# An S4D convolution with a routed MLP: merged loads for the last 64 channels of the gate and up weights, and products of constants ahead of the blocks that finish the last two channel groups

## The chip, the cores and the metric

The kernel runs on one core of one Trainium2 chip. The core has a matrix engine (TensorE, PE in the profile, with its weight loads on a row PEld), a vector engine (VectorE, DVE), a scalar engine (ScalarE, ACT), a general engine (GpSimd, POOL), and a sync engine (SyncE, SP) that only issues transfers; 16 DMA engines move data between HBM and the on-chip memory SBUF of 128 rows. TensorE writes to the eight banks of PSUM. The metric is the device time of one execution in microseconds; lower is better.

## The reference, cut to what matters

```
L, D, N, F = 2048, 576, 128, 4608
mod = (silu(c) @ w_mod)                       # sa, ca, ga, sb, cb, gb: six rows of 576
h = layernorm(x) * (1 + ca) + sa
# first half: S4D, a long convolution of every channel along the 2048 positions
A = -exp(log_A_real) + 1j * A_imag ;  dt = exp(log_dt) ;  C = (C_real + 1j * C_imag) * dt
K = 2 * einsum("dn,dnl->dl", C, exp(A * dt * pos)).real      # one filter per channel
y = irfft(rfft(h.T, 4096) * rfft(K, 4096))[:2048].T + h * D_skip
x = x + ga * y
# second half: a SwiGLU MLP for the 8 tokens with the highest router score
h = layernorm(x) * (1 + cb) + sb
r = h @ w_r ;  idx = argsort(-r)[:8] ;  s = h[idx]
z = ((silu(s @ w_gate) * (s @ w_up)) @ w_down) * sigmoid(r[idx])
x = x + gb * (h with z added at rows idx)
```

w_gate and w_up are 576 x 4608, w_down is 4608 x 576, all in 32-bit floats.

## The kernel before, in words

The 576 channels are worked in five groups, four of 128 channels and one of 64 (`GS`). For each group the filter is built, and the convolution is done as a two-level Fourier transform with TensorE products. Function `conv` (L944 on) multiplies the spectra of one part of a group and transforms back on one level (L1020); the copies at L1027 bring the result, z, from PSUM to a tile `zs`, and a store puts it into the DRAM tensor `dZ` (L1030). Function `y_group(g, jb)` then finishes quarter `jb` of the positions of group `g`: two loads bring z back from `dZ` in another order into a tile `zr` (L1052), eight TensorE products with the constant `g1` turn it into positions (L1061, 16 instructions in the trace, since each product is two passes), and VectorE adds the result to the residual `hx` (written by the helper `tt`, so the trace shows it at L342 as `hx<-b,hx`). There are two buffers of `zr`, so a load waits for the products of the block two before. When groups 2 and 4 are done, statistics (L1072) and sums for the router (L1079, L1092 on POOL, L1096 on ACT) follow for each quarter.

Then come the second normalization (`norm2`, small VectorE steps), the choice of the eight tokens (L1331 to L1367), the gathering of their rows (`px`, L1386, and L1409) into the tile `xT`, and the MLP: L1476 for gate and up, L1489 for a transpose, L1504 for down. Beside it, `base` scales all rows by the normalization and stores them (tiles `zr` again and `hx`, stores at L1455 on ACT's queue, four stores of 32 rows each for two token columns); its first four pairs use TensorE (L1449, L1450). At the end a scatter adds the MLP's rows (L1518).

The weights of the MLP are 45 tiles of up to 128 rows x 1536 numbers: for each of three parts s of F, four tiles each of gate and up with 128 channels (`g`, `u`), and one, `x`, that holds the last 64 channels of gate in rows 0 to 63 and those of up in rows 64 to 127; then 18 of w_down (`d`). `load_w` issues them on SP's queue in this order into 24 slots (`SLOTS`). The last eleven slots (`w2`) can only be filled when the convolution's memory is free, and the first of these loads also waits for the two small copies on POOL at L1139. An `x` tile is filled by two transfers (L1129, L1130).

The order of the work on each engine is written by a planner (`Plan`) from costs that stand in the code; the tables of priorities in `ORDER` belong to it. Each step has a planned cost and PSUM banks by name; a bank goes to a step in the planner's order, and on the chip the step waits until the bank's last reader is done. The change alters no planned cost, so the order stays. Waits on the chip are by semaphores; an engine works its list in order.

Of the kernel before, what the change touches and what calls it, by code (L numbers as in the profile page):

```python
# [310 lines left out]
def layouts(x):  # L311

    f = np.ascontiguousarray
    par = np.stack([x[n].T for n in ("A_C_real", "A_C_imag", "A_A_imag", "A_log_A_real")], 1)
    ld = np.zeros((128, NDT), np.float32)
    ld[:64] = x["A_log_dt"].reshape(64, NDT)
    dsk = np.zeros((128, KB, 4), np.float32)
    dsk[::32] = x["A_D_skip"].reshape(KB, 4, 4).transpose(2, 0, 1).reshape(4, KB, 4)
    cw = np.zeros((640, 1 + 6 * D), np.float32)
    cw[:D, 0], cw[:D, 1:] = x["c"][0], x["w_mod"]  # L320
    cw = cw.reshape(5, 128, 1 + 6 * D).transpose(1, 0, 2)
    return {"u": f(x["A_u"][0].reshape(32, 4, 16, D).transpose(1, 0, 2, 3).reshape(128, 16, D)),
            "par0": f(par[:, :, 0:GS[0]]), "par1": f(par[:, :, GS[0]:]),
            "head": f(np.concatenate([ld, cw[:, :, 0], dsk.reshape(128, 4 * KB)], 1)),
            "wm": f(cw[:, :, 1:].reshape(128, 5, 6, D).transpose(2, 0, 1, 3)),
            "wr": x["B_w_r"], "wg": x["B_w_gate"], "wu": x["B_w_up"], "wd": x["B_w_down"]}


@with_exitstack
def adaln_s4d_mod_kernel(ctx, tc, u, par0, par1, head, wm, wr, wg, wu, wd, cs, cfg, cr, cmv, out):  # L330
    nc = tc.nc
    V, S, P, T, Q = nc.vector, nc.scalar, nc.gpsimd, nc.tensor, nc.sync
    AX = mybir.AxisListType.X
# [66 lines left out]
    def banks(shape, names):  # L400
        return [ps.tile(shape, F32, name=nm) for nm in names]
# [4 lines left out]
    csm = const.tile([128, 128 + 128 + 32 + 16 + 1], F32, name="csm")  # L406
    ident = csm[:, 0:128]
# [538 lines left out]
    def conv(g, dp):  # L946
# [76 lines left out]
        for a in range(2):  # L1023
# [8 lines left out]
            ZS[x].rearrange("p (k e) -> p k e", e=n)), r=[("zsp", x, 0), ("zsp", x, 1)], inst=[("zs", x)],  # L1032
           w=[("dZ", g, dp)], dma=225, tag=f"y{g}")

    def y_group(g, jb):
        n = GS[g]
        gs = slice(GO[g], GO[g] + n)
        last = g >= G - 2
        if n == 128:
            ring("zr", (g, jb), 2)  # L1040
        elif not jb:
            ring("zr", (g, 0), 2)
            ring("zr", (g, 1), 2)
        jz = jb if n == 128 else jb // 2
        for m in range(2):
            s0 = 12 - 4 * jb if m == 0 else 4 * jb

            def lz(e, m=m, s0=s0):
                if (g, jz) not in ZT:
                    ZT[g, jz] = POOLS["z"].tile([128, 2, D], F32, name="zr", bufs=2)  # L1050
                ZR[g, jb, m] = flat(ZT[g, jz][:, m] if n == 128 else ZT[g, jz][:, jb % 2, 4 * n * m:4 * n * m + 4 * n], 4, n)
                (S if last and (n == 128 or not m) else Q).dma_start(ZR[g, jb, m], dZ[g][m, s0:s0 + 4].rearrange("s c h k e -> (c h k) s e"))  # L1052
            LX["z", g, jb] = op("A" if last and (n == 128 or not m) else "Q", .5, lz, r=[("dZ", g, dp) for dp in range(n // 16)],
                                w=[("zrp", g, jb, m)], inst=[("zr", (g, jz))], dma=290 if n == 128 else 190)
        st = {}

        def f(e, nm):
            st["p"] = py = banks([128, 4, n], nm)[0]
            for j4 in range(4):
                for m in range(2):  # L1060
                    T.matmul(py[64 * m:64 * m + 64, j4], g1[:, m], ZR[g, jb, m][:, 3 - j4 if m == 0 else j4],  # L1061
                             start=True, stop=True)
        m = op("T", .9 if n == 128 else .55, f, mode="1h", r=["csm"] + [("zrp", g, jb, m) for m in range(2)],
               inst=[("zr", (g, jz))], bank=1)
        op("V", vc(4 * n), lambda e: tt(hx[:, 4 * jb:4 * jb + 4, gs], st["p"], hx[:, 4 * jb:4 * jb + 4, gs], OP.add), uses=[m],
           w=[("y", g, jb)])
        if g not in (2, 4):
            return
        i, c0, c1 = (0, 0, 384) if g == 2 else (1, 384, D)
        yr = [("y", x, jb) for x in range(3 * i, g + 1)]  # L1070
        for j in range(4 * jb, 4 * jb + 4):
            op("V", vc(c1 - c0), lambda e, j=j: V.bn_stats(st2[:, j, i], hx[:, j, c0:c1]), r=yr, w=[("st2", i, j)])  # L1072

            def rd(e, j=j):
                yj = POOLS["z"].tile([128, 384], F16, name="yj")
                stt(yj[:, 0:c1 - c0], hx[:, j, c0:c1], 1.0, vrow[:, c0:c1], OP.mult, OP.mult,
                    accum_out=racc[:, j, i:i + 1])
            if i and j % 2 or not i and j < 8:
                op("V", vc(c1 - c0) + .13, rd, r=yr + ["vrow"], w=[("racc", i, j)], lock=True)  # L1079
                continue  # L1080
            kr = ring("pq", j, 2) if i else ring("pj", j, 1)
            sj = {}

            def pm_(e, j=j, sj=sj):
                if i:
                    if "pq" not in ZT:
                        ZT["pq"] = POOLS["z"].tile([128, 384], F32, name="pj", bufs=1)
                    sj["t"] = ZT["pq"][:, 192 * (j // 2 % 2):192 * (j // 2 % 2) + 192]
                else:
                    sj["t"] = POOLS["z"].tile([128, 384], F32, name="pj", bufs=1)  # L1090
                tt(sj["t"], hx[:, j, c0:c1], vrow[:, c0:c1], OP.mult, P)
            op("P", .6 if i else 1.08, pm_, r=yr + ["vrow"] + [("racc", 0, x) for x in range(8, 16)] * i, w=[("pj", i, j)], inst=[kr],  # L1092
               lock=True)

            def am_(e, j=j, sj=sj):
                S.activation(sj["t"], sj["t"], AF.Copy, accum_out=racc[:, j, i:i + 1])  # L1096
            op("A", ac(c1 - c0) + .12, am_, r=[("pj", i, j)], w=[("racc", i, j)], inst=[kr])
# [6 lines left out]
    def load_w(i):  # L1104
        s_, nm, k = key = order[i]
        sl = SLOTS[i % len(SLOTS)]
        rk = ring(sl, ("w", i), SLOTS.count(sl))

        def f(e):
            if sl[:2] == "sp":  # L1110
                w = spx[:, 1536 * int(sl[2]):1536 * int(sl[2]) + 1536]
            elif sl == "E":
                w = tw.tile([128, 3, 512], F32, name="E", bufs=NE).rearrange("p a d -> p (a d)")
            elif sl == "SC":
                w = tw.tile([128, 2, 2, 512], F32, name="SC", bufs=2).rearrange("p a b d -> p (a b d)")[:, 0:1536]
            else:
                w = W.pop("h", None) or W[sl].tile([128, 1536], F32, name="w")
            wtile[key] = w
            if nm == "d":
                f0 = 1536 * (k // 2) + 512 * s_ + 256 * (k % 2)  # L1120
                Q.dma_start(w[:, 0:2 * D].rearrange("p (r n) -> p r n", n=D),
                            wd[f0:f0 + 256].rearrange("(r p) n -> p r n", r=2))
                return
            w = w.rearrange("p (c x) -> p c x", c=3)

            def cols(x, r0, r1):
                return x[r0:r1].rearrange("p (c s x) -> p s c x", c=3, s=3)[:, s_]
            if nm == "x":
                Q.dma_start(w[0:64], cols(wg, 512, 576))  # L1129
                Q.dma_start(w[64:128], cols(wu, 512, 576))  # L1130
            else:
                Q.dma_start(w, cols(wg if nm == "g" else wu, 128 * k, 128 * k + 128))
        if i == SLOTS.index("w2"):
            r_ = [("zrp", G - 1, jb, m) for jb in range(4) for m in range(2)]

            def hold(e):
                W["h"] = W[sl].tile([128, 1536], F32, name="w")
                for n_ in range(2):
                    P.tensor_copy(W["h"][0:1, 8 * n_:8 * n_ + 8], ZR[G - 1, 3, n_][0:1, 0, 0:8])  # L1139
            op("P", .3, hold, r=[sl] + r_[6:], w=[("w", key)], inst=[rk, ("zr", (G - 1, 1))])  # L1140
        op("Q", .9 if nm == "x" else .45, f, r=[sl] if sl[0] == "w" else [], w=[("w", key)], inst=[rk],
           dma=495 if nm == "d" else 670)
        WK[key] = rk
# [47 lines left out]
    for x in (4, 3, 5):  # L1191
# [10 lines left out]
       w=["wrow"], **lk)  # L1202
# [29 lines left out]
    for b in range(KB):  # L1232
# [8 lines left out]
        g = group(b)  # L1241
# [101 lines left out]
    def pc(e, nm):  # L1343
# [5 lines left out]
       w=["i2"])  # L1349
# [5 lines left out]
       w=["pos", "jk"], lock=True)  # L1355
# [4 lines left out]
       w=["rsel", "jk"], lock=True)  # L1360
    op("A", .25, lambda e: S.activation(ft("rcol", [128, 1]), pk(2), AF.Sigmoid, bias=sc2[:, 1:2]), r=["rsel", "wrow"],
       w=["rcol"], table="sig")
    op("V", .1, lambda e: V.tensor_copy(ft("icol", [128, 1], I32), pk(1)), r=["idp"], w=["icol"])

    def pb(e, nm):
# [6 lines left out]
       w=["oh8"])  # L1372
# [90 lines left out]
    for s_ in range(3):  # L1463
# [22 lines left out]
        def tr(e, nms, st=st):  # L1486
# [5 lines left out]
           w=[("hT", s_)])  # L1492
# [19 lines left out]
    for c in range(4):  # L1512
# [6 lines left out]
        out=out[0], out_offset=bass.IndirectOffsetOnAxis(ap=ft("icol", None)[0:8, :1], axis=0), in_=ft("yo0", None)[0:8],  # L1519
# [24 lines left out]
```

## Time and profile before

| | |
|---|---|
| median of 3 runs | 483.56 us (483.1 to 487.92) |
| profiled execution | 484.27 us |
| its span, first to last instruction | 482.5 us |
| mean granted TensorE clock | 0.928 |
| busy: PE, PEld, DVE, ACT, POOL | 408.1, 285.2, 357.2, 318.7, 241.8 us |
| read from HBM, written | 71.94 MB, 23.62 MB |

A row of the timeline gives the start in us from the span's first instruction, the length, engine, line, operation, output and inputs, shape, a count, and in brackets how long the engine had been idle and what ended that. `SPq` and `ACTq` are issues of transfers on these engines' queues. A row of the windows gives for a stretch its length, each engine's busy time with the count of instructions, the granted TensorE clock (1.00 is full), the share of the DMA engines' time that was busy, and GB/s. In names like `b` (PSUM), buffer numbers are left out. Line numbers are those of the kernel before.

### The profile page before, as it was taken

The numbers are of one execution on the slowest core, as the hardware profiler recorded it, in microseconds if no ns is written. First come the engines' busy times: TensorE is split into PE (matmuls) and PEld (weight loads), VectorE is DVE, ScalarE is ACT, GpSimd is POOL, SyncE is SP. The second block draws the span as 40 slices with busy tenths as digits, with TensorE's granted clock in tenths as the row PEclk, the third lists the DMA queues.
The fourth block names the chain that finished last, engine by engine and source line by source line (L and its number), as shares of the span: only waits on it lengthen the run. The fifth ranks groups of instructions, "written<-read, shape, count | busy, mean of one in ns | idle before, by whom it ended". The sixth has DMA issues, their size and how long they took to land. (4 is left out here: it accounts for less than half of the span.)

```text
span 482.5 us, 15984 instructions
## 1 busy us (share of the span) xinstructions
PE 408.1 (85%) x6757; PEld 285.2 (59%) x6757; DVE 357.2 (74%) x751; ACT 318.7 (66%) x600; POOL 241.8 (50%) x206
## 2 busy tenths in 40 slices
PE   2968579969979889998899999999999869979474
PEld 1634335434547566866577777688798757543153
DVE  6898986899767877678896679688797859864121
ACT  5598966664897999999899989876622222252210
POOL 0006633022055788947758699956545533213931
PEclk9998966898999999999999999999999966998869
DMA  8995000476669522206432322575999777999993
GB/s 319 436 375 203 1 1 2 126 194 170 186 197 350 204 90 90 67 24 176 154 95 73 100 82 88 167 241 154 316 311 343 254 197 277 335 349 337 410 401 110
DMA packets 73388, 96.58 MB, mean 200 GB/s; under 512 B 12251, under 2 KB 45403, under 8 KB 72166
## 3 DMA queue, kind: packets, MB, share of 16 engines
q1 hardware_dynamic: 63686, 85.06, 53.8%
q10 hardware_dynamic: 9600, 10.49, 6.3%
q8 instruction: 53, 0.87, 0.8%
q14 instruction: 17, 0.14, 0.1%
q0 software_dynamic: 32, 0.02, 0.0%
HBM read 71.94 MB, written 23.62 MB: 198 GB/s over the span
## 5 line engine op out<-in xcount | busy, mean ns | idle before, releaser
L342 POOL TENSOR_TENSOR SC<-SC,E 128x1024 f32<-128x1024 f32 x36 | 86.1, 2394 | 98.6 <-ACT SC L851 54.4
L342 POOL TENSOR_TENSOR t<-t 128x256 f32<-128x256 f32 x72 | 55.1, 769 | 28.9 <-DVE t L342 23.3
L342 POOL TENSOR_TENSOR E<-E,SC 128x1024 f32<-128x1024 f32 x23 | 54.8, 2382 | 11.6 <-PE b L636 7.4
L342 DVE TENSOR_TENSOR t<-b,us 128x512 f32<-128x512 f32 x72 | 47.0, 685 | 12.6 <-PE b L970 9.6
L336 DVE TENSOR_SCALAR n<-b 128x512 f16<-128x512 f32 x72 | 46.9, 682 | 8.0 <-PE b L821 7.9
L844 ACT ACTIVATE SC<-b 128x512 f32<-128x512 f32 x72 | 42.1, 604 | 11.8 <-PE b L892 5.2
L1020 PE MATMUL b<-t,fg 64*128 64x128 f32 (+1 forms) x640 | 44.9, 281 | 2.9 <-issue 1.1
L1020 PEld LDWEIGHTS b<-t,fg 64*128 64x128 f32 x640 | 39.7, 187 | 9.1 <-issue 6.0
L795 ACT ACTIVATE E<-b 128x512 f32<-128x512 f32 x72 | 40.5, 606 | 3.4 <-PE b L791 3.2
L846 ACT ACTIVATE SC<-b 128x512 f32<-128x512 f32 x72 | 41.8, 598 | 0.2
L970 PE MATMUL b<-xk,fg 128*64 128x128 f32 (+1 forms) x640 | 38.5, 267 | 1.6 <-ACT zs L1027 0.8
L970 PE MATMUL b<-xu,fg 128*64 128x128 f32 (+1 forms) x640 | 37.3, 265 | 2.9 <-issue 1.0
L892 PE MATMUL b<-Bc,SC 128*32 128x64 f32 x1152 | 36.7, 224 | 1.8 <-DVE s L771 0.7
L970 PEld LDWEIGHTS b<-xk,fg 128*64 128x64 f32 x640 | 31.7, 137 | 10.5 <-issue 3.6
L342 POOL TENSOR_TENSOR zr<-zr,ksb 128x576 f32<-128x576 f32 x14 | 20.4, 1470 | 33.6 <-ACT zr L1435 27.0
L970 PEld LDWEIGHTS b<-xu,fg 128*64 128x64 f32 x640 | 32.2, 137 | 8.4 <-issue 1.8
L1435 ACT ACTIVATE zr<-hx,rs 128x576 f32<-128x576 f32 x16 | 12.9, 859 | 35.6 <-DMA out<-zr 16.8
L892 PE MATMUL b<-E,SC 128*32 128x64 f32 x1152 | 35.9, 222 | 0.3 <-DVE E L342 0.3
L912 PE MATMUL b<-csf,ksb 128*64 128x128 f32 x576 | 35.4, 275 | 0.3 <-DVE Bc L339 0.2
L892 PEld LDWEIGHTS b<-Bc,SC 128*32 128x32 f32 x1152 | 27.0, 111 | 12.6 <-issue 7.7
L912 PEld LDWEIGHTS b<-csf,ksb 128*64 128x64 f32 x576 | 31.2, 137 | 4.7 <-issue 1.5
L342 DVE TENSOR_TENSOR Bc<-E,b 128x512 f32<-128x512 f32 x36 | 24.5, 681 | 11.6 <-PE b L892 3.6
(251 smaller groups left out, 906.5 us busy)
## 6 DMA issues: line engine op xcount, KB each, us to landing
dX<-xs SPq DMA_DIRECT2D x32, 288.0 KB, 4.0
xu<-dX SPq DMA_DIRECT2D x36, 256.0 KB, 3.8
wt<-in_wm SPq DMA_DIRECT2D x6, 1440.0 KB, 15.1
w<-in_wu SPq DMA_DIRECT2D x9, 768.0 KB, 9.2
w<-in_wd SPq DMA_DIRECT2D x11, 576.0 KB, 8.6
w<-in_wg SPq DMA_DIRECT2D x8, 768.0 KB, 7.1
dZ<-zs SPq DMA_DIRECT2D x24, 256.0 KB, 2.3
zr<-dZ SPq DMA_DIRECT2D x24, 256.0 KB, 4.6
```

The source lines that it names most:

```text
L336: (eng or V).tensor_scalar(o, a, s1, s2, op0=op0, **({"op1": op1} if op1 is not None else {}))
L342: (eng or V).tensor_tensor(o, a, b, op=op)
L795: op("A", .49, lambda e, h=h: S.activation(tile_()[:, 1 + h], st["p"][h], AF.Exp), uses=[m], w=[("E", b, 1 + h)], inst=[("E", b)], table=" ...
L844: op("A", .49, lambda e, h=h: S.activation(sct()[:, h, 0], B_[h], AF.Abs), uses=[mm_[h]], r=[("ph", b, h)], w=[("ab", b, h)], inst=[("SC", ...
L846: op("A", .49, lambda e, h=h: S.activation(sct()[:, h, 1], B_[h], AF.Sin, scale=TWO_PI), uses=[mm_[h]], r=[("ph", b, h), ("ab", b, h)], w= ...
L892: T.matmul(kp[32 * t4:32 * t4 + 32, x], sc()[:, h, ri, 0, 32 * i:32 * i + 32], mo[ri][:, h, :, 32 * i:32 * i + 32], start=ri == 0, stop=ri ...
L912: T.matmul(o[64 * cc:64 * cc + 64, :, 4 * x:4 * x + 4].rearrange("p k j -> p j k"), ksb[:, b % KS, x], c1k[:, cc], start=True, stop=True)
L970: T.matmul(p[64 * a:64 * a + 64, q, cc], f2(k0 + k)[:, cc], src(k), start=True, stop=True)
L1020: T.matmul(pz[a][:, q], g2(k0 + 2 * q + cc)[r], pr[r, q, cc], start=cc == 0, stop=cc == 1, tile_position=(64 * a, 0))
L1435: op("A", ac(576), lambda e, j=j: S.activation(tile_(j), hx[:, j], AF.Identity, bias=rs[:, j, 1:2], scale=rs[:, j, 0:1]), r=[("rs2", j), ( ...
```

## The change

Two things are changed. The host lays out the last 64 channels of gate and up once more as an input `wx` of shape 3 x 128 x 1536, in the order in which an `x` tile holds them, and `load_w` fills an `x` tile by one transfer of 128 rows with 6144 contiguous bytes each instead of two transfers of 64 rows with three pieces of 2048 bytes each. And in `y_group`, for groups 3 and 4, three products (group 3) or two (group 4) of the constant identity with the first 256 columns of the constant tile `csm` are written into the block's PSUM tile before its eight products, which then overwrite it.

```diff
 def layouts(x):
     f = np.ascontiguousarray
+    runs = lambda w: f(w.reshape(-1, 3, 3, 512).transpose(2, 0, 1, 3).reshape(3, -1, 1536))
...
-            "wr": x["B_w_r"], "wg": x["B_w_gate"], "wu": x["B_w_up"], "wd": x["B_w_down"]}
+            "wr": x["B_w_r"], "wg": x["B_w_gate"], "wu": x["B_w_up"], "wx": runs(np.concatenate([x["B_w_gate"][512:], x["B_w_up"][512:]])), "wd": x["B_w_down"]}
...
+    def fill(p, n):
+        T.matmul(p.rearrange("p a b -> p (a b)")[:, 0:n], ident, csm[:, 0:n], start=True, stop=True)
+
     def y_group(g, jb):
...
         def f(e, nm):
             st["p"] = py = banks([128, 4, n], nm)[0]
+            for x in range((3 if n == 128 else 2) if g > 2 else 0):
+                fill(py, 256)
             for j4 in range(4):
                 for m in range(2):
                     T.matmul(py[64 * m:64 * m + 64, j4], g1[:, m], ZR[g, jb, m][:, 3 - j4 if m == 0 else j4],
...
+            if nm == "x":
+                Q.dma_start(w, wx[s_])
+                return
             w = w.rearrange("p (c x) -> p c x", c=3)

             def cols(x, r0, r1):
                 return x[r0:r1].rearrange("p (c s x) -> p s c x", c=3, s=3)[:, s_]
-            if nm == "x":
-                Q.dma_start(w[0:64], cols(wg, 512, 576))
-                Q.dma_start(w[64:128], cols(wu, 512, 576))
-            else:
-                Q.dma_start(w, cols(wg if nm == "g" else wu, 128 * k, 128 * k + 128))
+            Q.dma_start(w, cols(wg if nm == "g" else wu, 128 * k, 128 * k + 128))
```

More of the change, by code (lines that the diff above doesn't have):

```diff
@@ L325, in layouts, with adaln_s4d_mod_kernel @@
             "wm": f(cw[:, :, 1:].reshape(128, 5, 6, D).transpose(2, 0, 1, 3)),
-            "wr": x["B_w_r"], "wg": x["B_w_gate"], "wu": x["B_w_up"], "wd": x["B_w_down"]}
+            "wr": x["B_w_r"], "wg": x["B_w_gate"], "wu": x["B_w_up"], "wx": runs(np.concatenate([x["B_w_gate"][512:], x["B_w_up"][512:]])), "wd": x["B_w_down"]}
 @with_exitstack
-def adaln_s4d_mod_kernel(ctx, tc, u, par0, par1, head, wm, wr, wg, wu, wd, cs, cfg, cr, cmv, out):
+def adaln_s4d_mod_kernel(ctx, tc, u, par0, par1, head, wm, wr, wg, wu, wx, wd, cs, cfg, cr, cmv, out):
     nc = tc.nc
```

## The prediction

> **What bounds the kernel now.** I read the chain of waits first, from its end backwards. The profiled execution took 484.27 us around a span of 482.5, so 1.77 us lie outside the span.
>
> ```profile
> 384.14 1.05 PE b L1061 x16
> 410.26 0.88 ACT zr L1435
> 422.86 5.86 DMA out<-zr
> 433.25 4.45 PE b L1476 x32
> 437.72 8.44 DMA w<-in_wd
> 463.75 10.17 DMA w<-in_wd
> 473.94 3.51 DMA out<-hx
> ```
>
> Columns: start, length, what. Three stages are seen. To about 400 us the products of L1061 and the additions behind them end the last two groups. From 410 to 433 a chain of small steps runs the second normalization and the choice of the tokens, with stores of `out` in it (5.86 us for one). From 437.72 to the end it is weights arriving. So I ask two things: when does the tail at L1061 end, and how fast do weights flow after 437. The windows answer the second. The columns end with granted clock, DMA share and GB/s:
>
> ```profile
> 362.00:366.00 4.00, 4.00 (x80) 3.65 (x78) 3.45 (x7) 0.82 (x3) 2.34 (x4) 1.00 1.04 230
> 410.00:414.00 4.00, 2.86 (x18) 1.76 (x16) 2.81 (x9) 3.14 (x4) 1.88 (x2) 1.00 1.05 213
> 414.00:419.00 5.00, 4.95 (x17) 2.79 (x17) 4.33 (x14) 0.00 (x0) 0.94 (x1) 1.00 1.04 385
> 436.00:442.00 6.00, 6.00 (x80) 2.09 (x76) 2.08 (x3) 0.87 (x1) 2.80 (x2) 0.93 0.96 274
> 442.00:470.00 28.00, 18.23 (x271) 9.46 (x267) 7.71 (x11) 7.53 (x11) 16.09 (x11) 0.76 1.04 403
> ```
>
> The DMA engines are full in all five, but they move 385 to 403 GB/s in two and 213 to 274 in the others. The slow ones follow the issues of the half-tiles, whose two loads (L1129, L1130) each write 64 of the 128 rows:
>
> ```profile
> 399.40 0.55 SPq L1132 DMA_DIRECT2D w<-in_wu  x1
> 402.34 0.67 SPq L1129 DMA_DIRECT2D w<-in_wg  x1
> 403.06 0.60 SPq L1130 DMA_DIRECT2D w<-in_wu  x1
> 434.49 0.55 SPq L1129 DMA_DIRECT2D spx<-in_wg  x1
> ```
>
> Full tiles are cut in the same pieces of 512 numbers (L1132), so I blame the 64 rows, not the piece.
>
> For the first question, TensorE in the tail (start, length, idle before it and releaser):
>
> ```profile
> 384.07 1.09 PE L1061 MATMUL b<-zr,csm 128*64 128x128 f32 x16
> 386.33 1.09 PE L1061 MATMUL b<-zr,csm 128*64 128x128 f32 x16 [1.17 <-issue]
> 389.01 1.92 PE L1061 MATMUL b<-zr,csm 128*64 128x128 f32 x16 [1.58 <-DMA zr<-dZ]
> 391.71 2.46 PE L1061 MATMUL b<-zr,csm 128*64 128x128 f32 x16 [0.79 <-DVE hx L342]
> 394.95 1.98 PE L1061 MATMUL b<-zr,csm 128*64 128x64 f32 x32 [0.78 <-DVE hx L342]
> 398.15 1.98 PE L1061 MATMUL b<-zr,csm 128*64 128x64 f32 x32 [1.23 <-DMA zr<-dZ]
> ```
>
> The first four rows are the four blocks of group 3, the last two hold two blocks each of group 4. The same 16 instructions take 1.09 us, then 1.92 and 2.46: the granted clock halved.
>
> ```profile
> 385.70:389.11 3.41, 1.20 (x18) 1.01 (x20) 3.38 (x9) 1.23 (x4) 1.46 (x2) 1.00 0.78 238
> 389.11:406.18 17.07, 13.76 (x108) 10.84 (x108) 11.03 (x43) 4.26 (x18) 6.17 (x11) 0.50 0.70 200
> 409.59:413.01 3.42, 2.28 (x17) 1.53 (x16) 2.19 (x9) 2.75 (x4) 1.05 (x1) 1.00 1.06 229
> 430.08:433.49 3.41, 1.51 (x20) 0.88 (x16) 2.28 (x6) 2.51 (x4) 1.07 (x1) 1.00 0.76 234
> 433.49:436.90 3.41, 3.41 (x28) 1.23 (x24) 3.05 (x7) 0.98 (x2) 1.59 (x2) 0.50 1.03 360
> ```
>
> After a stretch with TensorE busy 1.20 of 3.41 us (35%) or 1.51 (44%) the clock is at 0.50; after one with 2.28 (67%) it stayed.
>
> **The change: the added products.** One product of the identity with 256 columns is priced by its like, with 288 columns at full clock:
>
> ```profile
> 406.38 0.65 PE L1449 MATMUL b<-ksb,csm 128*128 128x288 f32 x2
> 406.87 0.65 PE L1450 MATMUL b<-hx,csm 128*128 128x288 f32 x2
> ```
>
> They start 0.49 us apart; times 256/288 gives 0.43. Three cost 1.3 us, two 0.87; at half clock 2.6 and 1.73. In all 20 products, 8.6 us at full clock. They read only constants, so they don't wait for z; but they write the block's own PSUM tile, so they wait for whatever freed it. Two rows above wait for `DVE hx`, the addition of the block before: there the bank is the gate. So I walk the tail with the additions of VectorE:
>
> ```profile
> 385.21 0.69 DVE L342 TENSOR_TENSOR hx<-b,hx 128x512 f32<-128x512 f32 x1 [1.51 <-PE b L1061]
> 385.82 0.75 DVE L1027 COPY zs<-b 128x256 f32<-128x256 f32 x2
> 387.46 0.69 DVE L342 TENSOR_TENSOR hx<-b,hx 128x512 f32<-128x512 f32 x1
> 390.96 0.69 DVE L342 TENSOR_TENSOR hx<-b,hx 128x512 f32<-128x512 f32 x1 [1.73 <-PE b L1061]
> 394.20 0.69 DVE L342 TENSOR_TENSOR hx<-b,hx 128x512 f32<-128x512 f32 x1 [2.55 <-PE b L1061]
> 397.12 0.41 DVE L342 TENSOR_TENSOR hx<-b,hx 128x256 f32<-128x256 f32 x1
> 400.17 0.42 DVE L342 TENSOR_TENSOR hx<-b,hx 128x256 f32<-128x256 f32 x1 [0.23 <-PE b L1061]
> ```
>
> Block 0 of group 3 starts without idle and its z was loaded long before: its three products cost their full 1.3, and the addition moves from 385.21 to 386.5. VectorE is in order, so the last copies of zs move to 387.1, and with them their store and the z loads of group 4. Block 1 started just after the first of those copies ended (385.82 and half of 0.75, 386.2), so I take that copy as what freed its bank: products from 387.6 to 388.9, block to 390.0, addition at 390.1 (+2.6). Block 2's z waits for block 0's buffer (+1.3, from 389.0 to 390.3); its bank comes free at 390.8; products to 392.1, block (1.09, if the clock holds) to 393.2, addition at 393.3 (+2.3: the clock gives back 0.83). Block 3: bank at 394.0, products to 395.3, z about 394.9 (its row is 0.54 longer than the one before, so it came about 392.25; plus 2.6), block to 396.4, addition 396.5 (+2.3). Group 4 at full clock takes 0.55 a block: first block 397.2 to 398.6, second to 400.0 (addition 400.05 for 397.12, +2.9), third waits for that addition and ends about 402.0, fourth 403.4. The last addition moves from 400.17 to 403.4, **+3.2 us**.
>
> Behind it VectorE runs without a gap to the ACT row at 410.26: the normalization moves by the same 3.2. The weight stream's start hangs on POOL:
>
> ```profile
> 396.69 2.30 POOL L342 TENSOR_TENSOR pj<-hx,vrow 128x192 f32<-128x192 f32 x4 [6.51 <-DVE hx L342]
> 398.93 0.45 POOL L1139 COPY w<-zr 1x8 f32<-1x8 f32 x2
> ```
>
> The copies of L1139 let SP's load at 399.40 go. They stand behind four products of 0.575, of which the last two need the addition at 397.12: with 400.5 for its end the load goes at about 402.2 (+2.8).
>
> The row 385.70:389.11 bears on a rule. Its longest idle stretch is 1.58 us, and the clock fell. The Trainium skill, "TensorE: Matmul & The Clock Gate" (what's actually happening), has the clock fall after at least one idle window of about 3.4 us. By that rule the clock would not have fallen here, and after the change, whose gaps are about 1 us at most, it could not fall: the third rival below would have no chance. By the rows it can, so that rival keeps one. The sum is the same by both.
>
> **The change: one transfer for two.** A half-tile pair is 2 x 64 x 1536 x 4 bytes = 0.786 MB. Three pairs:
> - At 436 to 442, 6.00 us at 274 GB/s are 1.64 MB, 4.08 us at 403: 1.9 less; the pair alone, at 213 against 403, 3.69 against 1.95: 1.74. I take **-1.8**. The chain runs through weights from here, so it counts.
> - At 410 to 414, 0.852 MB, 2.21 us at 385: 1.8 less. But the chain there runs through VectorE and stores; the stream feeds it only by sharing the rings with the stores (5.86 us). Between 0 and -1.8; I take **-0.8**.
> - At 362 to 366 TensorE is busy 4.00 of 4.00, which hides it: 0. If that cover were gone it would be worth up to -1.7.
>
> SP issues one DMA instead of two (0.60 us less), idle time mostly. Fewer transfers in flight shift which earlier landing each later one waits for; no row prices that. The nearest are stores, 5.86 us among weights and 3.51 at the end: a wait that moves onto or off such a transfer is worth up to 2.35 either way. I take 0, the middle.
>
> Sum: +3.2 - 1.8 - 0.8 = +0.6, so 484.9 for an execution like the profiled one. That one lies 0.7 above the median of the three runs (483.56), so I forecast **484.2**, no change. About 1% (4.8 us, so 478.7 to 488.4) is what a measurement tells from no change.
>
> **Rivals.**
> *The waits swallow the products (0.3).* Idle before the six rows of L1061 is 1.17 + 1.58 + 0.79 + 0.78 + 1.23 = 5.55 us, and the clock returns 0.83 + 1.37 + 0.89 + 0.89 = 3.98. If all of it could be used, 8.6 products cost -0.9. With both pairs in full: 483.56 - 0.9 - 1.8 - 1.8 = 479.1. For: the idle is there. Against: block 0 has none, and the banks put the products behind the waits, not into them. That is 0.4 from the bound of 478.7, so I let half of this case pass it.
>
> *The halves are not what is slow (0.1).* If the rate comes from the source rows, one transfer is as slow: 484.2 + 2.6 = 486.8. Against: full tiles with equal pieces run at 385.
>
> *The clock falls all the same (0.09), and it is slower.* Blocks and products now alternate with waits of some 0.8 us for the bank: 2.4 busy of 3.2, or 75%. The fall is decided somewhere between 44% and 67% busy. If one 3.4 us stretch lands below, every block of the rest pays half clock: for blocks 2 and 3 of group 3, 2.6 + 1.92 each, for group 4 1.73 + 1.0 each, with the same bank waits: last addition about 412.9 instead of 400.17, end 483.56 + 12.7 - 2.6 = 493.7. The stretch 389.11:406.18 was 81% busy and stayed at half clock, so it would last. The Trainium skill, same page (a second HAM failure mode), tells of just this: short idle times between groups that cycle through PSUM banks make the clock oscillate. By that rule this rival would be the likelier; the stretch 409.59:413.01, with a gap of over 1 us and the clock kept, speaks against.
>
> **The numbers.** Forecast 0.51 (its own range 481.5 to 487), rivals 0.3, 0.1 and 0.09. Faster by over 1%: half of the first rival, 0.15. Slower: the third rival and the upper ends of the second, 0.12. Same: 0.73. The range leaves out 2 in 10: 478.8 (the waits swallow) to 488.3 (no gain from the halves, landings shifted against it).
>
> **What would show it.** The first block of group 3 shows a VectorE addition 1.3 us later against the end of L1020; the last addition to the normalization stays 10.1 us. The clock stays 1.00 through the tail, L1061 blocks take 1.09 each. No window with a full DMA share falls under 350 GB/s around the third group of weights. I am wrong if the products run before the banks are free, if the last addition does not move, or if what the half-tiles give back is taken by later landings.

## The result, and the profile after

The changed kernel takes 489.25 us (median of 6 runs, 487.3 to 493.23) beside 484.9 us for the kernel before (6 runs, 480.65 to 487.92): a ratio of 1.0138, 95% interval 1.0100 to 1.0176. It is slower by 1.4% (0.9% by the two medians), where no change was forecast (484.2 us, 478.8 to 488.3). The profiled execution took 493.23 us around a span of 491.1 us, the slowest of the six, 8.6 us over the span before. A ratio leaves out runs that lie over 1.5% above the fastest of their kernel, and the chance scatter of this kernel reaches that far (in the set of e9 to e11 that takes 18 of the 29 runs of the kernel before out), so below the medians of all runs stand beside it.

The tail first. TensorE in the changed kernel (start, length, idle before it and releaser); L1037 are the added products, two passes each, L1067 the blocks:

```profile
386.82 1.56 PE L1037 MATMUL b<-csm 128*128 128x256 f32 x6
388.31 1.09 PE L1067 MATMUL b<-zr,csm 128*64 128x128 f32 x16
390.62 1.53 PE L1037 MATMUL b<-csm 128*128 128x256 f32 x6 [1.22 <-DVE zs L1028]
393.97 1.56 PE L1037 MATMUL b<-csm 128*128 128x256 f32 x6 [0.79 <-DVE hx L343]
400.73 1.13 PE L1037 MATMUL b<-csm 128*128 128x256 f32 x4 [0.79 <-DVE hx L343]
401.79 0.69 PE L1067 MATMUL b<-zr,csm 128*64 128x64 f32 x16
402.41 1.13 PE L1037 MATMUL b<-csm 128*128 128x256 f32 x4
403.47 0.68 PE L1067 MATMUL b<-zr,csm 128*64 128x64 f32 x16
```

The products stand behind the waits (1.22 us for the copies of `zs`, 0.79 for the addition of the block before), not in them, as the prediction had it. But a head of three lasts from 386.82 to 388.31, 1.49 us, and one of two from 400.73 to 401.79, 1.06 us. The additions of VectorE:

```profile
383.34 0.67 DVE L343 TENSOR_TENSOR hx<-b,hx 128x512 f32<-128x512 f32 x1
389.45 0.69 DVE L343 TENSOR_TENSOR hx<-b,hx 128x512 f32<-128x512 f32 x1 [3.00 <-PE b L1067]
399.99 0.69 DVE L343 TENSOR_TENSOR hx<-b,hx 128x512 f32<-128x512 f32 x1 [2.69 <-PE b L1067]
408.15 0.42 DVE L343 TENSOR_TENSOR hx<-b,hx 128x256 f32<-128x256 f32 x1 [1.21 <-PE b L1067]
```

The first row is the last addition of group 2, which no part of the change touches; in the kernel before it is

```profile
380.58 0.67 DVE L342 TENSOR_TENSOR hx<-b,hx 128x512 f32<-128x512 f32 x1
```

I call **the tail** the time from this addition to the last one: 24.81 us (408.15 - 383.34) after 19.59 (400.17 - 380.58), so +5.2. The clock was kept. The windows over the tail, before and then after (length, busy times of PE, PEld, DVE, ACT and POOL, clock, DMA share, GB/s):

```profile
380.35:400.60 20.25, 14.23 (x192) 12.39 (x192) 12.87 (x35) 4.93 (x18) 8.60 (x15) 0.72 0.61 167
```

```profile
383.10:408.60 25.50, 20.88 (x232) 16.19 (x232) 12.91 (x35) 5.74 (x22) 9.29 (x16) 1.00 0.49 132
```

TensorE is busy 6.65 us longer at a clock of 1.00 instead of 0.72: the products take more than the clock gives back.

The 8.6 us of the span are then 2.76 us ahead of the tail (383.34 for 380.58), 5.2 in it, and 0.7 behind it: from the end of the last addition to VectorE's last instruction it is 81.84 us before and 82.51 after. In the first part the change touches only the first of the three loads, which TensorE's work hides; it begins with a stretch of half clock. PE busy, clock, DMA share and GB/s in the kernel before, in the changed one, and in a second profile of the kernel before (e5):

```profile
137.00:147.20 10.20, 8.16 (x198) 1.00 0.90 260
```

```profile
137.00:147.20 10.20, 9.02 (x161) 0.50 0.92 257
```

```profile
137.00:147.20 10.20, 8.96 (x162) 0.50 0.90 246
```

The unchanged kernel has this stretch in one execution and not in another, and in e5 its tail starts late too (382.81). So the stretch is chance, and the 2.76 us are not put to the change.

The end of the chain of waits in the changed kernel:

```profile
475.69 1.35 DVE hx L343 x2
477.06 0.32 ACTq L1460
481.00 3.81 DMA out<-hx
485.11 1.73 issue
```

Before, the chain's last pieces were two loads of `w<-in_wd` and a store. Now it comes through VectorE's last `hx` and the eight stores that ScalarE issues behind it; the weights are no longer in it there. Beside it another chain ends level: the last of these stores lands at 484.81, and TensorE's last products, 5.57 us without a gap, end at 485.23.

### The profile page after: what moved, and what is told of

Read it like the earlier page. It is cut to its first block, busy times and chain, and to the rows that moved or that the text cites. A ratio compares the mean times of both kernels' runs of the same rounds, so it can differ in the third digit from the quotient of the medians.

```text
span 491.1 us, 16054 instructions
## 1 busy us (share of the span) xinstructions
PE 415.1 (85%) x6797; PEld 290.3 (59%) x6797; DVE 356.3 (73%) x751; ACT 318.7 (65%) x600; POOL 241.8 (49%) x206
## 5 line engine op out<-in xcount | busy, mean ns | idle before, releaser
L893 PE MATMUL b<-Bc,SC 128*32 128x64 f32 x1152 | 38.3, 230 | 1.5 <-DVE s L772 0.7
L1440 ACT ACTIVATE zr<-hx,rs 128x576 f32<-128x576 f32 x16 | 12.9, 858 | 39.2 <-DMA out<-zr 18.2
L893 PE MATMUL b<-E,SC 128*32 128x64 f32 x1152 | 37.5, 227 | 0.3 <-DVE E L343 0.3
```

What stands on the lines that cost most here:

```text
L893: T.matmul(kp[32 * t4:32 * t4 + 32, x], sc()[:, h, ri, 0, 32 * i:32 * i + 32], mo[ri][:, h, :, 32 * i:32 * i + 32], start=ri == 0, stop=ri ...
L1440: op("A", ac(576), lambda e, j=j: S.activation(tile_(j), hx[:, j], AF.Identity, bias=rs[:, j, 1:2], scale=rs[:, j, 0:1]), r=[("rs2", j), ( ...
```

## The experiments

The theory after the result: the products cost 5.2 us because a head is dearer than its passes; the merged transfer gives some of it back. The rivals: the transfer costs time by what it shifts, or gives nothing. Three numbers are read from each run's profile: the tail; from the start of the last addition to the last packet of the weights of w_down ("weights"); from the end of the last addition to VectorE's last instruction ("end"). The addition lasts 0.42 us, so a column is compared with itself alone.

```
run                         median us (before beside it)  ratio, 95% interval       tail   weights  end
before                                                                              19.59  73.1     81.8
after                       489.25 (484.90)               1.0138, 1.0100 to 1.0176  24.81  71.8     82.5
e1  merged                  485.33 (483.11)               1.0064, 1.0028 to 1.0101  18.54  70.4     80.1
e2  products, two halves    490.02 (483.11)               1.0161, 1.0095 to 1.0228  24.81  75.7     83.0
e3  one product a head      486.17 (483.11)               1.0076, 1.0038 to 1.0114  20.02  72.2     81.6
e4  merged, own bank        482.98 (483.11)               0.9973, 0.9935 to 1.0012  18.32  71.9     82.0
e5  before again            484.88 (483.53)               0.9980, 0.9934 to 1.0027  20.12  74.8     82.4
e6  merged again            484.42 (483.53)               1.0033, 0.9988 to 1.0079  19.70  72.3     82.4
e7  halves, own bank        484.50 (483.53)               1.0031, 0.9991 to 1.0071  18.36  74.2     81.8
e8  new source, two halves  483.12 (483.53)               1.0011, 0.9962 to 1.0060  19.02  73.2     81.3
e9  e4, stores divided      483.16 (483.31)               1.0067, 1.0023 to 1.0112  18.05  71.9     82.0
e10 e7, stores divided      482.66 (483.31)               1.0063, 1.0016 to 1.0109  17.96  74.8     83.0
e11 before, stores divided  484.36 (483.31)               1.0071, 1.0005 to 1.0137  19.63  72.9     82.1
e12 e9, two stores later    481.59 (482.29)               0.9983, 0.9936 to 1.0030  18.57  72.3     82.3
e13 e10, two stores later   482.30 (482.29)               1.0023, 0.9978 to 1.0068  17.90  74.0     82.6
e14 products of 64 columns  489.32 (486.10)               one run each              23.07  71.4     81.4
```

**e1 and e6: the merged transfer alone.**

```diff
-            for x in range((3 if n == 128 else 2) if g > 2 else 0):
-                fill(py, 256)
```

> The merged transfer without the added products. Theory (the products cost about 5.2 us in the tail, more than the 3.2 predicted, because each head of three costs 1.49 us and not 1.30; the merged transfer gives some of it back): the tail is as before, 19.8 us from the start of the first multiplication of group 4's second half (L1021) to the last addition to hx, the time is 0 to 2 us below the kernel before (about 483.9). Rival (the products cost the 3.2 us that were predicted and the merged transfer costs time through shifted landings): 1 us or more above the kernel before (about 486).

> The merged transfer alone once more, with a second profile. In the first set its mean half-clock time (twice the span times one minus the clock) was 75.7 us against 64.9 for the kernel before. Rival S (the merged transfer itself brings TensorE into stretches of half clock): again about 75 us, 0.3 to 1% slower than before, and the profile shows the additional stretches after 410 us. Rival C (chance of the windows): about 65 us, no difference in time.

The time didn't fall in either run: the medians lie 2.2 and 0.9 us above the kernel before, the first on the side of the rival. The predicted gain of 2.6 us would be a ratio of 0.9946, under both intervals. The mean half-clock time was 75.7 and 70.6 us, beside 64.9 and 68.6 for the kernel before in the same sets, and in neither profile do stretches after 410 us explain it. So no gain is shown; whether there is a loss of up to 1% stays open, since the kernel before against itself (e5) lies 1.35 us apart in its medians.

**e2: the products alone**, the two lines of e1 with the old loads.

> The added products with the two half transfers. Theory: the tail takes 5 us more than before (24.8 to 25.1 us), and the time is 4.5 to 6 us above the kernel before (about 490); no stretch of half clock between the start of the tail and the normalization. Rival (only 3.2 us, the rest from the transfers): 3.2 us above (about 488).

The tail is 24.81 us as in the changed kernel, and the time 6.9 us above the kernel before. The products alone explain the loss, and the rival of e1, by which they cost 3.2 us, is out.

**e3: one product a head.**

```diff
-            for x in range((3 if n == 128 else 2) if g > 2 else 0):
+            for x in range(1 if g > 2 else 0):
```

> The changed kernel with one product at each head in place of three or two. Theory (a head costs one pass every 0.216 us and 0.41 us to drain before the block's first weights load, so one product costs 0.63 us, eight heads 5.0 us against 10.2 us): the tail grows by 2.2 to 2.7 us, the time is about 1.5 us above the kernel before. Rival (price 0.43 us a product, no drain): the tail grows by 1.3 us, the time is about the kernel before. If one product isn't enough to keep the clock up, blocks of 1.9 us come back and the tail grows by 4 us or more.

```profile
387.07 0.70 PE L1037 MATMUL b<-csm 128*128 128x256 f32 x2 [0.79 <-DVE hx L343]
387.70 1.09 PE L1067 MATMUL b<-zr,csm 128*64 128x128 f32 x16
```

The head takes 0.63 us as the theory said, though it is spent in two places: the second pass starts 0.32 us behind the first, and the block 0.31 us behind the second. Eight heads keep the clock at 1.00 through the tail. The tail grew by only 0.4 us, less than both expected: I had scaled the 5.2 us down by the length of the heads, but what the clock gives back was there in full. Of the 20 products, 12 bought nothing. The median lies 3.1 us above the kernel before, which the tail doesn't explain; e1, with the same transfer, has 2.2 of that without any product, and the rest stays open.

**e4 and e7: the products in a bank of their own.** No block's bank gates them, so they run in the waits. The edit is shown against the kernel before, without the helper `fill`; in e4 it replaces the loop of the changed kernel.

```diff
+            ns = {(3, 1): 2, (3, 2): 3, (3, 3): 1, (4, 0): 1, (4, 2): 2}.get((g, jb), 0)
+            sb = ps.tile([128, 1, 256], F32, name="b5") if ns else None
+            for x in range(ns):
+                fill(sb, 256)
             st["p"] = py = banks([128, 4, n], nm)[0]
```

> The merged transfer, and products that write a bank of their own which nothing reads, so that they run in the waits for z and for the bank: two, three and one ahead of the second to fourth block of group 3, one and two ahead of the first and third of group 4, none ahead of the others. Theory (what costs is where the products stand, not that they are there; the kept clock is worth about 1.8 us in the tail): clock 1.00 through the tail, group 3's blocks 1.1 us each, the last addition 1 to 2 us earlier in the tail than before, the time 2 to 4 us below the kernel before (about 482). Rival 1 (the waits, not the clock, set the end of each block): the blocks are shorter but the last addition comes within 0.5 us of the kernel before, the time is that of the merged transfer alone. Rival 2 (products overrun the waits, or are too few and the clock falls): the tail is 1 us or more longer than before.

> The products in a bank of their own, as in e4, with the two half transfers of the kernel before. If the merged transfer costs 2 us (e1), this one lies 2 us below e4, at about 481 us or 0.7% below the kernel before: faster than both kernels. If it doesn't, it lies at e4's time, 0 to 0.3% below the kernel before. The tail takes about 18.6 us, as in e4.

```profile
380.79 1.13 PE L1037 MATMUL b<-csm 128*128 128x256 f32 x4
382.04 1.09 PE L1069 MATMUL b<-zr,csm 128*64 128x128 f32 x16
383.06 1.56 PE L1037 MATMUL b<-csm 128*128 128x256 f32 x6
385.94 1.09 PE L1069 MATMUL b<-zr,csm 128*64 128x128 f32 x16 [1.32 <-DMA zr<-dZ]
386.97 0.70 PE L1037 MATMUL b<-csm 128*128 128x256 f32 x2
387.82 1.09 PE L1069 MATMUL b<-zr,csm 128*64 128x128 f32 x16 [0.15 <-DVE hx L343]
```

The products now follow the block before at once, the block still waits for z (1.32 us) or for the addition (0.15), and each takes 1.09 us. Over six profiles of this kind (e4, e7, e9, e10, e12, e13) the tail is 18.2 us in the mean, over six without products (before, e1, e5, e6, e8, e11) 19.4. In the six without, 3.0 to 11.1 us of the tail run at half clock; in all ten with products, of either kind, at most 0.3. So the kept clock is worth 1.2 us where it costs nothing. That is a quarter of a percent, and no run here shows it in the time: e4 and e7 have ratios on both sides of 1, and e7 isn't faster than e4.

**e5: the kernel before once more.** 

> The kernel before, unchanged, once more: what two sets of runs of the same kernel differ by, and a second profile. If the half-clock stretch at 134 to 147 us, which the five changed kernels so far all have and the first profile of the kernel before has not, is chance (where the 3.41 us windows fall), it can appear here. The ratio should be 1.00 within 0.4%; the mean half-clock time about 65 us.

It gave the row with half clock at 137 to 147 us above.

**e8: the new source, read by two transfers.**

```diff
-                Q.dma_start(w, wx[s_])
+                Q.dma_start(w[0:64], wx[s_, 0:64])
+                Q.dma_start(w[64:128], wx[s_, 64:128])
```

> The new source (one input with the last 64 channels of both weights, each row in one run of 6144 bytes), but read by two transfers of 64 partitions each, no added products. If e1's cost came with the single transfer (which earlier landing each later transfer waits for), this one takes the time of the kernel before. If it came with the new source, it takes e1's time (+2 us). For the rate: if 64 partitions a transfer are what is slow, the windows of these loads stay at 210 to 280 GB/s; if the pieces of 2048 bytes are, they rise to 380 or more.

The windows of the second group's last 64 channels, first e1 (one transfer of 128 rows), then e8 (two of 64):

```profile
408.00:410.00 2.00, 1.71 (x8) 0.99 (x6) 1.06 (x8) 0.77 (x1) 0.00 (x0) 1.00 1.06 421
```

```profile
409.00:411.00 2.00, 0.46 (x2) 0.01 (x1) 1.07 (x4) 1.64 (x3) 0.00 (x0) 1.00 1.01 210
```

Same source and pieces of 6144 bytes, and half the rate with full engines: the 64 rows are what is slow, not the pieces. The Trainium skill, "SBUF — State Buffer" (Door 1), has a transfer to rows 0 to 63 or 64 to 127 reach only half of the ports; the trace agrees, 210 against 421 GB/s. In time e8 is level with the kernel before, so the new source costs nothing that can be measured.

**e9, e10, e11: four of the last eight stores through SP.** The weights arrive earlier with the merged transfer and the end doesn't come earlier, so I looked for what stands behind them.

```diff
-            op("A", .45, lambda e, q=q: S.dma_start(ov[q, ...
+            op("A", .45, lambda e, q=q: (Q if i > 5 and q % 2 else S).dma_start(ov[q, ...
```

> e4 (merged transfer, products in a bank of their own), and of the last eight stores of hx, which ScalarE issues one behind the other, four go through SP's queue, idle by then. Theory (the gain of the merged transfer ends at ScalarE's queue of stores, 4.6 to 6.7 us long, and not at the weights): the stores are issued in about 2.5 us, the time from the last addition of the tail to the end falls from 82.0 us to about 80, and the time is about 2 us below e4 (481). Rival (the stores wait for landings, through whichever queue they go): within 0.5 us of e4.

> The same with the two half transfers (e7 and the divided stores). Theory: here the weights land 1.7 us later against the tail and become the bound, so that the time from the last addition to the end is about 81.5 us, 1.5 us above e9: only now the merged transfer is worth something. Rival: no difference between e9 and e10 beyond 0.5 us in that stage, as there was none between e4 and e7.

> The kernel before with the divided stores alone. Theory: as in e10, the weights' landings bound the end, 0 to 1 us gained, the time within 0.2% of the kernel before. Rival (the queue of stores is the whole bound): 2 us gained.

The ends of e9 and e11 stay within 0.3 us of e4 and the kernel before, that of e10 is 1.2 us above e7's. ScalarE's queue of stores was no bound of its own. e9 ends 1.0 us before e10, less than the 1.5 expected, and the medians show nothing: they differ from the kernel before by -0.15, -0.65 and +1.05 us, though the three ratios lie above 1, for the reason given with the result.

**e12, e13: two more stores out of ScalarE's way.** In the changed kernel ScalarE's first copy to `hT` stands behind a store that waits for a landing of weights (4.16 us here, 3.97 in e9):

```profile
471.28 0.32 ACTq L1460 DMA_DIRECT2D out<-hx  x1
471.64 0.48 ACT L1496 COPY ksb<-b 128x384 f32<-128x384 f32 x1 [4.16 <-DMA w<-in_wd]
```

```diff
+            def so(e, q=q):
+                if (i, q) in ((4, 1), (5, 2)):
+                    late.append((i, q))
+                    return
+                for i_, q_ in late if (i, q) == (6, 0) else []:
+                    Q.dma_start(ov[q_, :, 2 * i_:2 * i_ + 2], hx[32 * q_:32 * q_ + 32, 2 * i_:2 * i_ + 2])
...
```

> e9 (merged transfer, products in a bank of their own, four of the last eight stores through SP), and the two stores of hx that stand ahead of ScalarE's copies to hT are issued behind them, through SP. Theory (that store, which waits for a landing of w<-in_wd, holds hT back, and so the last products): ScalarE's idle time ahead of the first copy to hT falls from 3.97 us to about 1, hT is complete 2 to 3 us earlier, the last products wait for weights again, and the time from the last addition to the end falls from 82.0 to about 80 us. Rival (hT waits for products and weights ahead of it in any case): the idle time goes to another wait and the stretch stays within 0.5 us of 82.

> The same with the two half transfers (as e10). Theory: hT is earlier here too, but the weights land 2 to 3 us later against the tail than with the merged transfer and bound the end: 82 to 83 us from the last addition to the end, 1.5 us or more above e12. Rival: the same as e12 within 0.5 us.

The copy in e12, and the piece that then stands in the chain of waits:

```profile
460.43 0.48 ACT L1508 COPY ksb<-b 128x384 f32<-128x384 f32 x1 [1.58 <-PE b L1506]
```

```profile
462.64 9.54 DMA out<-hx
```

The wait fell from 3.97 to 1.58 us, and the second part's `ohz` follows the first's 2.4 us earlier (2.45 us behind it for 4.84). But a store now put on SP takes 9.54 us to land among the weights, later stores wait for it, and the end stays at 82.3 and 82.6 us. Each wait taken away here was followed by another landing. The rivals' number holds, one transfer or two, the end is the same; the reason given for it in e12 does not, since ScalarE's two copies to `hT` did come earlier, by 1.5 us against the last addition.

**e14: the products in the block's own shape**, the left 64 columns of the identity.

```diff
-        T.matmul(p.rearrange("p a b -> p (a b)")[:, 0:n], ident, csm[:, 0:n], start=True, stop=True)
+        T.matmul(p.rearrange("p a b -> p (a b)")[0:64, 0:n], ident[:, 0:64], csm[:, 0:n], start=True, stop=True)
```

> The changed kernel with the added products on the left 64 columns of the identity (128 rows, 64 columns, 256 numbers a product, the shape in which the block's own products use the array), three and two at each head as in the changed kernel. Theory (the 0.41 us behind the last pass are paid for the change from the full array to half of it): the head of three takes 1.30 us from its first product to the block's first, that of two 0.86, and the tail is about 24 us in place of 24.8. Rival (any product ahead of the block is drained): 1.49 and 1.06 again, the tail 24.8.

```profile
385.93 1.29 PE L1037 MATMUL b<-csm 128*64 128x256 f32 x5
386.85 0.43 PE L1067 MATMUL b<-zr,csm 128*64 128x128 f32 x2
387.06 0.38 PE L1037 MATMUL b<-csm 128*64 128x256 f32 x1
387.28 1.04 PE L1067 MATMUL b<-zr,csm 128*64 128x128 f32 x14
```

The block's first products, on the other half of the array, start at 386.85, ahead of the last pass at 387.06, and the rest goes on 0.22 us behind that pass, where after full-array products it was 0.31. The second pass starts 0.27 us behind the first, where it was 0.32. From the head's start to the block's end it is 2.39 us (385.93 to 388.32) for 2.58. The tail is 23.07 us, 1.7 less than in the changed kernel. So 0.19 us a head are paid for the change of shape; the other half's early start is not what gains them, since the half behind the products still ends the block. The Trainium skill, "TensorEngine Tiling (Array Packing)" (Key Properties), says that changing the tiling mode drains TensorE; the trace agrees: the block's first weight load starts 0.31 us behind the start of the last full-array pass, and in e14 together with the last pass.

## Why the prediction was wrong

**Where the products stand** was right: block 0 pays its head in full (its addition comes 1.49 us later against the products of L1020 ahead of it; 1.3 was predicted), the others start theirs when the bank is free. The clock stayed at 1.00, the blocks of group 3 take 1.09 us, the normalization starts 9.8 us behind the last addition (10.1 before), and the rivals "the waits swallow the products" and "the clock falls all the same" did not come true. The failure mode of the Trainium skill, "TensorE: Matmul & The Clock Gate" (A second HAM failure mode), by which short gaps between banks make the clock oscillate, didn't show either: it held at 1.00 over the tail's 25.5 us.

**Their size** is the first step that failed: "Three cost 1.3 us, two 0.87". The passes do come 0.216 us apart (0.43 a product), but the second of a head comes 0.32 us behind the first, and the block 0.31 us behind the last; so three cost 1.49 and two 1.06. That is 0.19 a head, 1.5 us over eight heads: the prediction priced the products among their own kind and put the change to them and back at nothing. The blocks of group 4 take 0.61 to 0.69 us where 0.55 was taken. Together that is about the 2.0 us by which the tail's +5.2 exceeds the +3.2. e14, without the 0.19, got 1.7 back.

**"The chain runs through weights from here, so it counts"** is the second. The merged transfer does what was said to the weights: over eight profiles with one transfer their last packet comes 71.8 us after the last addition, over eight with two 74.1, so 2.3 earlier (2.6 predicted). But the end comes at 81.7 (six profiles, stores undivided) and 82.1 us (five): 0.4 earlier, within a scatter of about 2 us. At 436 to 442, where the half tiles are slow, TensorE has no gap to close. The prediction's own window said so, 6.00 us busy of 6.00; by the same sign, 4.00 of 4.00 at 362 to 366, it had put the first pair at 0. The kernel before, then the changed one:

```profile
440.98 10.18 PE L1476 MATMUL b<-w,xT 128*32 128x384 f32 x128
451.09 0.88 PE L1476 MATMUL b<-spx,xT 64*32 64x384 f32 x16
459.02 0.90 PE L1489 MATMUL b<-csm,ohz 128*128 128x128 f32 x3 [7.06 <-DVE ohz L342]
```

```profile
448.26 10.18 PE L1481 MATMUL b<-w,xT 128*32 128x384 f32 x128
458.37 0.88 PE L1481 MATMUL b<-spx,xT 64*32 64x384 f32 x16
468.12 0.90 PE L1494 MATMUL b<-csm,ohz 128*128 128x128 f32 x3 [8.88 <-DVE ohz L343]
```

The gate and up products run back to back, 10.18 us in both; the slow half tiles of the third group were hidden by them. Behind them TensorE waits for `ohz`, which waits for ScalarE, which stands behind stores that wait for landings:

```profile
465.70 1.28 ACT L1486 ACT_TABLE_LOAD   x1 [1.73 <-DMA E<-in_wd]
466.49 0.32 ACTq L1460 DMA_DIRECT2D out<-hx  x1
```

That wait of TensorE is 8.88 us after and 7.06 before. All 16 profiles taken together show the same: counted from the start of the last addition, the gate and up products end 1.7 us earlier with one transfer (51.7 for 53.5 in the mean of eight each), and the first product on `ohz` starts only 0.3 earlier (60.1 for 60.3). Why a store waits for weights that it doesn't read stands in the trace: the one at 471.28 waits for semaphore 102, which it uses itself, and a load of weights issued at 463.04 had used it last. "I take 0, the middle" for shifted landings was thus the term to look at: the landings decide this stretch, with either number of transfers. "What the half-tiles give back is taken by later landings" was named as what would make the prediction wrong, and it is what happened. The chain before named a load there; that a load ends last doesn't show that the end moves with it.

**The rates** were right in the first two groups (312 and 385 GB/s at 362 to 366 in the changed kernel for 230 before; 421 in e1's second group for 210 with halves). In the third the promise of no window under 350 GB/s failed in the changed kernel, though e1's same transfer ran at 377:

```profile
444.00:446.00 2.00, 2.00 (x28) 0.78 (x24) 0.82 (x2) 0.00 (x0) 1.03 (x1) 1.00 0.84 183
```

```profile
435.00:437.00 2.00, 2.00 (x30) 0.79 (x25) 0.12 (x1) 0.00 (x0) 1.74 (x2) 1.00 1.00 377
```

Why is open; the DMA engines had less to do (0.84).

So +5.2 for the tail and about -0.4 for the transfers, where the sum had +3.2 and -2.6: near 4.8, and the medians differ by 4.35. That they agree so closely is luck, since medians of the unchanged kernel differ by 1.35 us (e5).

## What to carry to other kernels

Work that is to keep the clock up belongs into the waits, in a bank that gates nothing and in the shape of what follows; ahead of a block, in its own bank, three and two cost 5.2 us here and one each 0.4, and one did as much for the clock as three. What the kept clock gives, 1.2 us of the tail, no run here shows in the time, and no run has the products both in the waits and in the block's shape. Before a faster transfer is counted, look whether the reader waits for it: here TensorE's rows showed 10 us without a gap. A chain of waits names who came last, and next to it stood other waits of nearly the same length.

## What the runs showed of the hardware

The kernel before ranges from 476 to 489 us, and much of that is the clock: over the 75 runs of e1 to e4, the changed kernel and the kernel before beside e1 to e4, the span grows within each kernel by 0.23 us for each us of half clock, of which there were 40 to 83 us in the profiles. Stretches are multiples of 3.41 us, and the same code gets one or not from one execution to the next. In the changed kernel the clock fell after one idle window, behind the tail:

```profile
416.83:420.25 3.42, 0.02 (x1) 1.00 1.01 396
420.25:423.66 3.41, 3.41 (x14) 0.50 1.05 387
```

That is as the Trainium skill, "TensorE: Matmul & The Clock Gate" (What's actually happening), has it; but the kernel before fell after windows with 35% and 44% busy, in the rows of the prediction. Nor is the fall "decided somewhere between 44% and 67% busy", as the prediction took it. In e3's tail a window with 1.69 of 3.41 us busy (50%) kept the clock, and ahead of the stretch at 137 us the same work, busy 73% of the window, was followed by half clock in the changed kernel and by full clock in the kernel before:

```profile
133.53:136.94 3.41, 2.50 (x12) 1.00 0.23 54
136.94:140.35 3.41, 2.44 (x62) 0.50 0.98 274
```

```profile
133.11:136.53 3.42, 2.51 (x12) 1.00 0.22 55
136.53:139.94 3.41, 2.17 (x72) 1.00 0.95 273
```

What decides it, no run here shows.
